# A linear-attention and feed-forward kernel on one Trainium2 core: its static order, early transfers, early engines and feed-forward leads planned anew

## The chip, the cores and the metric

The kernel runs on one core of a Trainium2 chip. Its time is the device time of one execution in microseconds (us); the time before is the median of three runs. The engines are named as in the profile: PE (TensorE matmul), PEld (its weight loads), DVE (VectorE), ACT (ScalarE), POOL (GpSimd) and SP, whose queue starts the loads.

## What is computed

```python
def _attn_ref(q, k, v, alpha):              # each (4, 8, 768, 48)
    for t in range(S):
        state = alpha[:, :, t, :, None] * state + np.einsum('bhd,bhe->bhde', k[:, :, t], v[:, :, t])
        y[:, :, t] = np.einsum('bhd,bhde->bhe', q[:, :, t], state)
def _moe_ref(x, w1, w2, w3, w_out):         # x: (3072, 384) from y; w: (384, 768), w_out: (768, 384)
    h = np.maximum(np.maximum(x @ w1, x @ w2), x @ w3)
    return h @ w_out
```

All inputs and the output are float32.

## The kernel before

**Units.** The 768 positions are cut into 6 blocks of 128, and with 4 batches that makes 24 units (u); a unit has 8 heads of 48. Two units form a group n (12 groups), which shares its loads: four inputs a, q, k, v of 384 KB each (alpha, q, k, v), in five rotating buffers (`load`, L383).

**Attention of a unit** (`prep` L519, `output` L607, `state` L665). ACT takes the logarithm of alpha (L489); PE sums it over the block with a triangular matrix (L530); ACT takes two exponentials, ep and en (L533, L535). q times ep and k times en go to a 16-bit tile qk (L542, on POOL or DVE), v is scaled to 16 bits (L548 on ACT or L553 on POOL). PE turns q and k with eight transposes (L563), DVE copies them out of PSUM (L567), PE forms the scores (L575), DVE masks them (LA, L580), PE adds up the output (L618, L621), ACT scales it to xb (L638), PE turns xb (L645) and DVE copies it to xT (L649). The state is carried by L676 (PE), L682 (DVE) and L689 (DVE in the first block, POOL later).

**Feed-forward of a group** (`ffn`, L698). Since max(x w1, x w2, x w3) = x w1 + max(max(x (w2 - w1), x (w3 - w1)), 0) up to the order of terms, the kernel keeps wd = w2 - w1 and w3 - w1 (`subs`, L437) and the folded product w1 w_out (w1o; PE turns w1 in L454, multiplies in L471, ACT copies). PE multiplies wd with xT (L714; 36 matmuls of 128x256 a group), ACT applies relu (L724), DVE takes the maximum (L729), PE multiplies with w1o and w_out (L745; 9 matmuls of 128x384 a unit), ACT copies the result (L755) and starts its store (L756).

**The order.** No engine's order is written out by hand. Every operation is a `plan.step` with an engine, a cost, a rank, what it reads and writes, and for loads a transfer time (`load=`). `Plan.order` (L173) runs these steps once in a model of the engines, the transfers (`Transfers`, L52), the PSUM banks and PE's clock (`Clock`, L93): at each moment the step that can start first is taken, among equals that of the lowest rank. The result is the static order of each engine's queue; on the chip, an engine runs its queue strictly in that order and waits where an input is late. Units have rank u; group n's feed-forward has rank 2n + LEAD (L31, L702), so a larger lead lets attention go first. The constants at the head steer it: EARLY (L32) names the engines for q, k and v of the first units (POOL where nothing is said), SUBS (L37) those of the subtractions, WCUTS (L36) the pieces in which each weight matrix is loaded, FIRST (L39) the order of the first transfers on SP's queue, WARM (L46, `warm` L652) a number of matmuls on zeros that keep PE busy, PAIRS (L47) the unit from which the scores of two units are run as one step.

Of the kernel before, what the change touches and what calls it, by code (L numbers as in the profile page):

```python
# [10 lines left out]
FP32 = mybir.dt.float32  # L11
# [19 lines left out]
LEAD = 5.0  # L31
EARLY = {0: ("POOL", "POOL", "POOL"), 1: ("DVE", "POOL", "ACT"), 2: ("DVE", "DVE", "POOL"),  # L32
         3: ("DVE", "POOL", "POOL"), 4: ("POOL", "DVE", "POOL"), 5: ("DVE", "DVE", "ACT"),
         6: ("POOL", "POOL", "POOL"), 7: ("DVE", "POOL", "ACT"), 8: ("POOL", "DVE", "POOL")}
WEIGHTS = ()
WCUTS = (0, 256, 512, 768)  # L36
SUBS = {(1, 0): "POOL", (1, 1): "DVE", (1, 2): "DVE", (2, 0): "POOL", (2, 1): "POOL",  # L37
        (2, 2): "POOL"}
FIRST = (("a", 0, 0, 1), ("w", 1, 0), ("q", 0, 0, 1), ("a", 0, 1, 2), ("w", 0, 0),  # L39
         ("k", 0, 0, 1), ("q", 0, 1, 2), ("w", 1, 1), ("k", 0, 1, 2), ("w", 2, 0), ("w", 0, 1),  # L40
         ("v", 0, 0, 1), ("v", 0, 1, 2), ("w", 2, 1), ("w", 1, 2), ("a", 1, 0, 1),
         ("q", 1, 0, 1), ("w", 2, 2), ("w", 0, 2), ("k", 1, 0, 1), ("akq", 1, 1, 2),
         ("w", 3, 1), ("w", 3, 0), ("v", 1, 0, 1), ("w", 3, 2), ("v", 1, 1, 2),
         ("aqkv", 2, 0, 2), ("aq", 3, 0, 1), ("q", 3, 1, 2), ("k", 3, 0, 1), ("a", 3, 1, 2),
         ("v", 3, 0, 1), ("v", 3, 1, 2), ("k", 3, 1, 2))
WARM = (2, 1, 9)  # L46
PAIRS, CROSS = 8, 99  # L47
TURNED, PAUSE = 3.5, 0.3
# [3 lines left out]
class Transfers:  # L52
# [6 lines left out]
    def add(self, e, arrival, work, i, late):  # L59
        self.jobs[e].append([arrival, work, i, late])  # L60

# [55 lines left out]
class Plan:  # L117
# [12 lines left out]
    def step(self, eng, cost, rank, run, reads=(), writes=(), banks=(), load=0.0, line=None,  # L130
             mode=0, late=0.0, after=0.0):
        i = len(self.steps)
        deps = set()
        if line is not None:
            if line in self.tail:
                self.behind[i] = self.tail[line]
            self.tail[line] = i
        for k in reads:
            if k in self.writer:
                deps.add(self.writer[k])  # L140
        for k in writes:
            if k in self.writer:
                deps.add(self.writer[k])
            deps.update(self.readers.get(k, ()))
        for k in reads:
            self.readers.setdefault(k, []).append(i)
        for k in writes:
            self.writer[k] = i
            self.readers[k] = []
        deps.discard(i)  # L150
        for k in set(reads) | set(writes):
            if k in self.users:
                self.users[k].append(i)
        for k in banks:
            self.users[k] = [i]
        self.steps.append((eng, cost, rank, run, deps, tuple(banks), load, mode, late, after))
# [16 lines left out]
    def order(self):  # L173
# [23 lines left out]
        dma, mode = Transfers(), 0  # L197
# [17 lines left out]
        while len(seq) < n:  # L215
            best = None
            for e, cand in pending.items():
                pick = None
                for i in cand:
                    at = self.homes(bank_free, self.steps[i][5])  # L220
                    if at is None:
                        continue
                    t = max(ready[i], free[e], at[0])
                    turn = TURN_RANK if e == "PE" and self.steps[i][7] != mode else 0.0
                    key = (t, self.steps[i][2] + turn, i)
                    if pick is None or key < pick:
                        pick = key
                if pick is not None and (best is None or pick < best[0]):
                    best = (pick, e)
            landing = dma.next()  # L230
# [6 lines left out]
            _, cost, _, _, _, banks, load, m, late, after_ = self.steps[i]  # L237
# [12 lines left out]
            if load:  # L250
                dma.add(e, t + cost + DMA_IN[e], load, i, late)
            else:
                finish(i, t + cost + HOP[e] + after_)
# [7 lines left out]
def kernel(  # L261
# [30 lines left out]
    NX = 6  # L292
# [42 lines left out]
    xTs = homes(NX, [P, NFT, TG], FP16, "xT")  # L335
    hTs = homes(3, [P, NJ, TG], FP16, "hT")
# [46 lines left out]
    def load(n, lo, hi, names="aqkv"):  # L383
        cb, g = divmod(n, B // UB)
        for x in names:
            t = ld[x][n % 5]

            def run(x=x, t=t):
# [6 lines left out]
                      load=(1.84 if n < 3 else 2.02 if n < CROSS // 2 else 2.02 + PAUSE) * (hi - lo) / HG,  # L395
# [21 lines left out]
    def wload(g, part):  # L417
# [6 lines left out]
                  load=3.2 * (WCUTS[part + 1] - WCUTS[part]) / DF)  # L424
# [93 lines left out]

    def prep(u):  # L519
# [39 lines left out]
        def trans():  # L559
            live[tk] = bank(tk, [P, 2, NP, P], FP16)  # L560
            for w in range(2):
                for j in range(NP):
                    nc.tensor.transpose(live[tk][:, w, j, :], qk[:, w, 2 * j:2 * j + 2, :], ident)  # L563

        plan.step("PE", 0.45, u, trans, banks=[tk],
                  reads=[("qk", u % 7, 0), ("qk", u % 7, 1)], writes=[tk, ("qkT room", u % 3)])
        plan.step("DVE", 0.69, u, lambda: nc.vector.tensor_copy(out=qkT, in_=live[tk]),  # L567
                  reads=[tk], writes=[("qkT", u % 3)])
# [38 lines left out]
    def output(u):  # L607
# [20 lines left out]
        if u >= CROSS:  # L628
            def across():
                nc.scalar.activation(out=xb, in_=live[yk].rearrange("p a b -> p (a b)"),  # L630
                                     func=AFT.Copy, scale=ysc)
                nc.scalar.dma_start_transpose(out=xTs[n % NX][:, :, i * P:(i + 1) * P], in_=xb)

            plan.step("ACT", 0.93, u, across, reads=[yk], after=TURNED,
                      writes=[("xb", u % 5), ("xT", n % NX, i)])
            return
# [3 lines left out]
                  reads=[yk], writes=[("xb", u % 5)])  # L640

        def turn():
            live[xk] = bank(xk, [P, NFT, P], FP16)
            for ft in range(NFT):
# [4 lines left out]
                  lambda: nc.vector.tensor_copy(out=xTs[n % NX][:, :, i * P:(i + 1) * P], in_=live[xk]),  # L649
                  reads=[xk], writes=[("xT", n % NX, i)])  # L650

    def warm(u, w, count):  # L652
        live["wm"] = None

        def zeros():
            live["wm"] = bank(("wm", 0), [P, TG], FP32)
            nc.tensor.matmul(live["wm"], Zs[1][0].rearrange("p a b -> p (a b)")[:, :P],
                             Zs[1][0].rearrange("p a b -> p (a b)")[:, :TG], start=True, stop=True)

        for i in range(count):  # L660
            plan.step("PE", 0.11, 90.0, zeros, banks=[("wm", 0)] if i == 0 else [], line="warm",
                      reads=[("qk", u % 7, w)] if i == 0 else [],
# [35 lines left out]
    def ffn(n):  # L698
        cb, g0 = divmod(n, B // UB)
        xT, hT = xTs[n % NX], hTs[n % 3]  # L700
        npieces = 2 * (NJ // 2) + UB
        rank = [2 * n + LEAD + 2.0 * i / npieces for i in range(npieces)]  # L702
        for j in range(NJ // 2):
            parts = parts_of(j)
            for g in range(2):
                r = rank[2 * j + g]
                gk = ("gp", n, j, g)

                def grow(j=j, g=g, gk=gk):
                    live[gk] = bank(gk, [P, 2, TG], FP32)  # L710
                    for jj in range(2):
                        c0 = (2 * j + jj) * P
                        for kt in range(NFT):
                            nc.tensor.matmul(live[gk][:, jj, :], wd[:, kt, g, c0:c0 + P],  # L714
                                             xT[:, kt, :], start=(kt == 0), stop=(kt == NFT - 1))

                plan.step("PE", 0.656, r, grow, banks=[gk],
                          writes=[gk] + ([("room", n % 3, j)] if g == 0 else []),
                          reads=[("room", n % 3, j)] * (g > 0)
                          + [("wd", g + 1, p) for p in parts] + [("xT", n % NX, 0), ("xT", n % NX, 1)])  # L720
                h = hT[:, 2 * j:2 * j + 2, :]
                if g == 0:
# [3 lines left out]
                              reads=[gk], writes=[("hT", n % 3, j)])  # L726
                else:
                    plan.step("DVE", 0.69, r,
                              lambda h=h, gk=gk: nc.vector.tensor_max(h, live[gk], h),  # L729
                              reads=[gk, ("hT", n % 3, j)], writes=[("hT", n % 3, j)])  # L730
        for i in range(UB):
            b = g0 * UB + i
            m = n * UB + i
            r = rank[2 * (NJ // 2) + i]
            ok = ("op", m)
            nk = NFT + NJ
            parts = [(0, nk)] if n < NG - 1 else [(0, nk - 2), (nk - 2, nk)]
            for lo, hi in parts:
                def shrink(i=i, ok=ok, lo=lo, hi=hi):
                    if lo == 0:  # L740
                        live[ok] = bank(ok, [P, DM], FP32)
                    for kt in range(lo, hi):
                        a, w = ((xT[:, kt], w1o[:, kt]) if kt < NFT
                                else (hT[:, kt - NFT], wo16[:, kt - NFT]))
# [5 lines left out]
                          reads=[(x, n % 3, j) for x in ("hT", "room")  # L750
                                 for j in range(max(0, lo - NFT) // 2, (hi - NFT) // 2)]
                          + [("xT", n % NX, i)] + [("w", 3, p) for p in range(nparts)] + [("w1o", kt) for kt in range(NFT)])
# [5 lines left out]
            plan.step("ACT", 0.9, r, leave, reads=[ok], writes=[("ob room", m % 4)])  # L758


    for what, n, lo, *hi in FIRST:
# [4 lines left out]
        else:  # L766
            load(n, lo * H, hi[0] * H, what)
    made = dict.fromkeys(SUBS, False)
    for n in range(NG):
# [21 lines left out]
        if n >= 4:  # L791
            ffn(n - 4)
    for n in range(NG - 4, NG):
        ffn(n)
# [35 lines left out]
```

## Time and profile before

| what | us |
|---|---|
| median of 3 runs (156.71 to 157.77) | 157.55 |
| the profiled execution | 157.7 |
| its span, first to last instruction | 155.9 |
| PE busy | 137.4 |
| DVE busy | 100.6 |
| ACT busy | 86.7 |
| POOL busy | 73.6 |
| last load landed (v of the last group) | 115.95 |
| last matmul ended | 151.6 |
| mean granted TensorE clock | 0.989 |

Times in the trace count from the start of the span; 1.8 us of the execution lie outside it. 23.69 MB are read and 4.72 MB written. A row of the timeline or of the groups names the line, the engine, the operation, the tiles it writes and reads, and in brackets the idle time of the engine ahead of it with what ended it.

### The profile page before, as it was taken

The page shows a single profiled execution, that of the slowest core. Times are in us where ns is not written, and L with a number is a line of the kernel's source. Part 1 is how long each engine was busy: PE and PEld are TensorE (multiplying, and loading weights), DVE is VectorE, ACT ScalarE, POOL GpSimd, SP SyncE. Part 2 cuts the span into 40 slices and gives each one's busy share as a digit, 9 for nine tenths or more (in the row PEclk, how much of TensorE's full clock was granted, in tenths as well). Part 3 has the DMA queues.
Part 4 walks back from the last instruction along what each step waited for, and adds up shares of the span by engine and source line. Part 5 has one row for each costly group of instructions (what it writes and reads, how often), then busy time and mean ns, then how long its engine had stood idle before and what let it go on. Part 6 is the DMA issues. An engine that isn't in the chain of part 4 may idle for free.

```text
span 155.9 us, 4070 instructions
## 1 busy us (share of the span) xinstructions
PE 137.4 (88%) x1621; PEld 106.8 (69%) x1621; DVE 100.6 (65%) x171; ACT 86.7 (56%) x175; POOL 73.6 (47%) x100
## 2 busy tenths in 40 slices
PE   0255695999999999999999999999999999999990
PEld 0133464676787797697787887787887877968750
DVE  7035529862998799873969685695884975833220
ACT  3462664679578583487366477284682653525221
POOL 0268704322144077597979548668469483000000
PEclk9999999599999999999999999999999999999999
DMA  5999998999998999998999989999961102011202
GB/s 139 247 277 290 290 294 176 320 204 229 191 236 172 220 254 178 231 276 167 249 254 201 269 184 240 231 217 197 269 136 53 48 4 101 4 50 50 87 13 101
DMA packets 107442, 28.66 MB, mean 184 GB/s; under 512 B 100000, under 2 KB 107424, under 8 KB 107424
## 3 DMA queue, kind: packets, MB, share of 16 engines
q1 hardware_dynamic: 103680, 23.60, 72.9%
q10 hardware_dynamic: 3744, 4.82, 8.9%
q8 instruction: 12, 0.20, 0.5%
q14 instruction: 6, 0.05, 0.1%
HBM read 23.69 MB, written 4.72 MB: 182 GB/s over the span
## 4 chain that ended last, share of the span: by engine, by line
PE 68%; DMA 12%; SPq 11%; ACT 2%; issue 2%; POOL 1%; DVE 1%; ACTq 0%; POOLq 0%
PE psum L714 26%; PE psum L745 19%; DMA an<-in_alpha_dram 7%; SPq L419 7%; PE psum L563 5%; DMA vn<-in_v_dram 4%; SPq L389 4%; PE psum L575 4%; PE psum L621 2%; PE psum L645 2%; PE psum L530 2%; PE psum L676 2%; PE psum L618 2%; POOL qk L542 1%; PE psum L502 1%
## 5 line engine op out<-in xcount | busy, mean ns | idle before, releaser
L714 PE MATMUL psum<-xT,wd 128*128 128x256 f16 x432 | 57.8, 283 | 0.0
L714 PEld LDWEIGHTS <-wd 128*128 128x128 f16 x432 | 42.0, 101 | 8.0 <-issue 1.0
L542 POOL TENSOR_TENSOR qk<-qn,ep 128x384 f16<-128x384 f32 x19 | 19.0, 1000 | 27.4 <-ACT ep L533 21.3
L580 DVE TENSOR_TENSOR LA<-psum,c 128x1024 f16<-128x1024 f32 x24 | 28.6, 1219 | 4.6 <-PE psum L575 4.6
L729 DVE TENSOR_TENSOR hT<-psum,hT 128x512 f16<-128x512 f32 x36 | 24.4, 687 | 10.9 <-PE psum L714 6.3
L724 ACT ACTIVATE hT<-psum 128x512 f16<-128x512 f32 x36 | 21.2, 603 | 13.1 <-PE psum L714 12.5
L745 PE MATMUL psum<-wo,hT 128*128 128x384 f16 x144 | 27.3, 326 | 0.0
L542 POOL TENSOR_TENSOR qk<-kn,en 128x384 f16<-128x384 f32 x20 | 20.0, 1000 | 7.6 <-ACT en L535 4.2
L755 ACT COPY ob<-psum 128x384 f32<-128x384 f32 x24 | 11.5, 478 | 20.9 <-PE psum L745 20.4
L567 DVE COPY qkT<-psum 128x1024 f16<-128x1024 f16 x24 | 16.4, 688 | 9.6 <-ACT ob L755 7.1
L745 PEld LDWEIGHTS <-hT 128*128 128x128 f16 x144 | 14.1, 98 | 9.3
L553 POOL TENSOR_SCALAR v<-vn,c 128x384 f16<-128x384 f32 x21 | 13.0, 622 | 13.6 <-DMA vn<-in_v_dram 12.2
L489 ACT ACTIVATE la<-an 128x768 f16<-128x768 f32 (+1 forms) x15 | 10.7, 715 | 14.0 <-DMA an<-in_alpha_dram 13.6
L563 PE MATMUL psum<-c,qk 128*128 128x128 f16 x192 | 16.2, 227 | 1.9 <-DVE qk L542 1.4
L689 POOL TENSOR_TENSOR Z<-U,G 48x192 f16<-48x192 f32 x32 | 15.7, 505 | 2.1 <-DVE U L682 1.2
L638 ACT ACTIVATE xb<-psum,c 128x384 f16<-128x384 f32 x24 | 13.8, 584 | 3.9 <-PE psum L621 2.2
L745 PE MATMUL psum<-w1o,xT 128*128 128x384 f16 x72 | 15.6, 326 | 0.0
L563 PEld LDWEIGHTS <-qk 128*128 128x128 f16 x192 | 12.6, 101 | 4.2 <-DVE qk L542 1.6
L533 ACT ACTIVATE ep<-psum 128x384 f32<-128x384 f32 x24 | 11.8, 494 | 4.4 <-PE psum L530 4.4
L649 DVE COPY xT<-psum 128x384 f16<-128x384 f16 x24 | 8.4, 353 | 7.5 <-PE psum L645 7.4
L530 PE MATMUL psum<-la,c 128*128 128x384 f16 x24 | 8.3, 345 | 4.6 <-ACT la L489 4.6
L621 PE MATMUL psum<-v,LA 128*128 128x48 f16 x192 | 11.5, 186 | 0.9 <-DVE LA L580 0.8
(41 smaller groups left out, 155.4 us busy)
## 6 DMA issues: line engine op xcount, KB each, us to landing
out_dram<-ob ACTq DMA_DIRECT2D x24, 192.0 KB, 3.1
ws<-in_moe_w_dram SPq DMA_DIRECT2D x9, 384.0 KB, 4.7
an<-in_alpha_dram SPq DMA_DIRECT2D x9, 384.0 KB, 6.1
qn<-in_q_dram SPq DMA_DIRECT2D x9, 384.0 KB, 6.3
kn<-in_k_dram SPq DMA_DIRECT2D x9, 384.0 KB, 5.6
vn<-in_v_dram SPq DMA_DIRECT2D x9, 384.0 KB, 6.4
an<-in_alpha_dram SPq DMA_DIRECT2D x6, 192.0 KB, 4.7
qn<-in_q_dram SPq DMA_DIRECT2D x6, 192.0 KB, 4.5
```

Of the source, the lines that this page charges most:

```text
L542: nc.gpsimd if eng == "POOL" else nc.vector).tensor_mul(
L553: lambda: nc.gpsimd.tensor_scalar(out=v16, in0=ld["v"][n % 5][:, hs], scalar1=vsc, scalar2=1.0, op0=AOP.mult, op1=AOP.mult),
L563: nc.tensor.transpose(live[tk][:, w, j, :], qk[:, w, 2 * j:2 * j + 2, :], ident)
L567: plan.step("DVE", 0.69, u, lambda: nc.vector.tensor_copy(out=qkT, in_=live[tk]), reads=[tk], writes=[("qkT", u % 3)])
L580: lambda: nc.vector.tensor_mul(LA.rearrange("p a b t -> p (a b) t"), live[Ak].rearrange("p a (b t) -> p (a b) t", t=P), maskA.unsqueeze(1) ...
L621: nc.tensor.matmul(yp[:, 2 * j + p, :], LA[:, p, j, :], v16[:, 2 * j + p, :], start=(cb == 0), stop=True, skip_group_check=True)
L638: lambda: nc.scalar.activation(out=xb, in_=live[yk].rearrange("p a b -> p (a b)"), func=AFT.Copy, scale=ysc),
L689: eng.tensor_mul(Zn[rows, :, cols], U[rows, :, cols], G[rows, i * NP:(i + 1) * NP].unsqueeze(2).broadcast_to([D, NP, D]))
L714: nc.tensor.matmul(live[gk][:, jj, :], wd[:, kt, g, c0:c0 + P], xT[:, kt, :], start=(kt == 0), stop=(kt == NFT - 1))
L724: lambda h=h, gk=gk: nc.scalar.activation(out=h, in_=live[gk], func=AFT.Relu),
L729: lambda h=h, gk=gk: nc.vector.tensor_max(h, live[gk], h),
L745: nc.tensor.matmul(live[ok], a[:, i * P:(i + 1) * P], w, start=(kt == 0), stop=(kt == nk - 1))
```

## The change

It alters the constants that steer the order, some costs in the planner's model, and how feed-forward work is cut into calls. The operations, their shapes and their number stay, but for the weights' pieces (three a matrix become two, so twelve transfers, six casts and six subtractions become eight, four and four) and the matmuls on zeros (9 of 256 columns become 12 of 384, put early and no longer after unit 2's k). The weight pieces in `FIRST` are reordered among those of a, q, k and v: both halves of q and a of group 0 come first, and w3 comes last. All subtractions run on DVE. The q and k products of units 1, 3 and 5 to 10 that go to DVE, and the v of units 8 to 10 that go to ACT, are chosen anew. Scores run in pairs from unit 12, not 8. The feed-forward lead 5.0 becomes 6.0 for the first call, 9.0 for the second and 7.0 for all others. The planner charges a store to the transfers (`store`), adds 1.0 us of other traffic at 24.5 us and every 11 us after, and costs a load of a group at 1.82 us each.

`turn_in` is the old code for turning q and k, moved into a function of its own. The new branches for turning by a transfer (`cross`, and the one in `output`) apply to units from 24 on, of which there are none; `WIDE` is 99, so feed-forward calls stay at two units. xT is held in 3 tiles of four units, not in 6 of two.

```diff
-LEAD = 5.0
-EARLY = {0: ("POOL", "POOL", "POOL"), 1: ("DVE", "POOL", "ACT"), 2: ("DVE", "DVE", "POOL"),
-         3: ("DVE", "POOL", "POOL"), 4: ("POOL", "DVE", "POOL"), 5: ("DVE", "DVE", "ACT"),
-         6: ("POOL", "POOL", "POOL"), 7: ("DVE", "POOL", "ACT"), 8: ("POOL", "DVE", "POOL")}
+LEAD = (6.0, 9.0, 7.0)
+EARLY = {1: ("POOL", "DVE", "POOL"), 3: ("DVE", "DVE", "POOL"), 4: ("POOL", "POOL", "POOL"),
+         5: ("DVE", "POOL", "POOL"), 6: ("DVE", "DVE", "POOL"), 7: ("POOL", "DVE", "POOL"),
+         8: ("POOL", "DVE", "ACT"), 9: ("POOL", "DVE", "ACT"), 10: ("POOL", "DVE", "ACT"),
+         11: ("POOL", "POOL", "POOL")}
-WCUTS = (0, 256, 512, 768)
-SUBS = {(1, 0): "POOL", (1, 1): "DVE", (1, 2): "DVE", (2, 0): "POOL", (2, 1): "POOL",
-        (2, 2): "POOL"}
-FIRST = (("a", 0, 0, 1), ("w", 1, 0), ("q", 0, 0, 1), ("a", 0, 1, 2), ("w", 0, 0),
-         ("k", 0, 0, 1), ("q", 0, 1, 2), ("w", 1, 1), ("k", 0, 1, 2), ("w", 2, 0), ("w", 0, 1),
-         ("v", 0, 0, 1), ("v", 0, 1, 2), ("w", 2, 1), ("w", 1, 2), ("a", 1, 0, 1),
-         ("q", 1, 0, 1), ("w", 2, 2), ("w", 0, 2), ("k", 1, 0, 1), ("akq", 1, 1, 2),
-         ("w", 3, 1), ("w", 3, 0), ("v", 1, 0, 1), ("w", 3, 2), ("v", 1, 1, 2),
+WCUTS = (0, 384, 768)
+SUBS = {(1, 0): "DVE", (1, 1): "DVE", (2, 0): "DVE", (2, 1): "DVE"}
+FIRST = (("aq", 0, 0, 1), ("aq", 0, 1, 2), ("k", 0, 1, 2), ("w", 0, 0), ("v", 1, 0, 1),
+         ("k", 0, 0, 1), ("k", 1, 0, 1), ("w", 0, 1), ("qa", 1, 0, 1), ("w", 1, 1),
+         ("w", 1, 0), ("v", 0, 0, 1), ("v", 0, 1, 2), ("k", 1, 1, 2), ("a", 1, 1, 2),
+         ("w", 3, 1), ("q", 1, 1, 2), ("w", 3, 0), ("w", 2, 0), ("v", 1, 1, 2), ("w", 2, 1),
...
-WARM = (2, 1, 9)
-PAIRS, CROSS = 8, 99
+WARM = (0, 0, 12)
+PAIRS, WIDE = 12, 99
+CROSS_IN, CROSS_OUT = 24, 24
+FETCH, FETCHES, STORE = 1.0, (24.5, 11.0), 0.3
...
+    def store(self, work):
+        if self.jobs["SP"]:
+            self.jobs["SP"][0][1] += work
...
-                      load=(1.84 if n < 3 else 2.02 if n < CROSS // 2 else 2.02 + PAUSE) * (hi - lo) / HG,
+                      load=1.82 * (hi - lo) / HG,
...
-                  load=3.2 * (WCUTS[part + 1] - WCUTS[part]) / DF)
+                  load=3.25 * (WCUTS[part + 1] - WCUTS[part]) / DF)
...
-    xTs = homes(NX, [P, NFT, TG], FP16, "xT")
+    xTs = homes(NX, [P, NFT, B * P], FP16, "xT")
...
-        rank = [2 * n + LEAD + 2.0 * i / npieces for i in range(npieces)]
+        rank = [u0 + LEAD[min(f, 2)] + k * i / npieces for i in range(npieces)]
```

In `FIRST`, an entry such as ("aq", 0, 0, 1) loads a and q of group 0, first unit of the two; ("w", 2, 1) loads the second piece of w3 (w1, w2, w3 and w_out count as 0 to 3).

## The prediction

> **What bounds the kernel now.** I read the page first: busy times, then the 40 slices.
>
> ```profile
> PE 137.4 (88%) x1621; PEld 106.8 (69%) x1621; DVE 100.6 (65%) x171; ACT 86.7 (56%) x175; POOL 73.6 (47%) x100
> ...
> PE   0255695999999999999999999999999999999990
> ...
> PEclk9999999599999999999999999999999999999999
> DMA  5999998999998999998999989999961102011202
> ```
>
> TensorE (PE) is full from slice 8 to the end; before that it waits, while the DMA engines are full from slice 2 until slice 29. So the kernel has two parts: a start of about 31 us whose pace is that of the transfers, and 120 us in which PE never rests. The stretches say how complete that is (columns: length, then busy time and instructions of PE, weight loads, DVE, ACT, POOL, then granted clock, DMA share, GB/s).
>
> ```profile
> 20.00:25.00 5.00, 4.32 (x23) 2.95 (x22) 1.94 (x3) 2.80 (x5) 1.34 (x1) 1.00 1.19 282
> 25.00:27.00 2.00, 1.07 (x16) 0.90 (x17) 2.00 (x3) 0.82 (x3) 0.29 (x1) 1.00 0.52 118
> 27.00:30.00 3.00, 3.00 (x22) 1.89 (x21) 2.74 (x5) 1.81 (x4) 0.99 (x1) 0.53 1.08 336
> 40.00:50.00 10.00, 10.00 (x139) 8.07 (x136) 8.66 (x17) 7.19 (x16) 3.81 (x5) 1.00 1.00 212
> 60.00:70.00 10.00, 9.68 (x124) 7.60 (x122) 8.40 (x14) 6.58 (x14) 7.25 (x13) 1.00 1.24 247
> ```
>
> After 40 us PE is idle for 0.7 us in all, up to the last matmul at 151.6. What the end is made of, then, is the column of PE's work plus what PE has lost by the time it is full. Third, the timeline, for how the start loses time:
>
> ```profile
> 20.23 3.87 PE L714 MATMUL psum<-xT,wd 128*128 128x256 f16 x18
> ...
> 23.71 2.00 DVE L542 TENSOR_TENSOR qk<-kn,en 128x384 f16<-128x384 f32 x1 [2.16 <-DMA kn<-in_k_dram]
> ...
> 25.76 0.40 PE L563 MATMUL psum<-c,qk 128*128 128x128 f16 x4 [1.45 <-DVE qk L542]
> ...
> 26.68 2.27 PE L714 MATMUL psum<-xT,wd 128*128 128x256 f16 x12
> ...
> 31.43 1.15 PE L657 MATMUL psum<-Z 128*128 128x256 f16 x9
> ```
>
> The 18 matmuls at 20.2 stand 0.213 us apart; later ones 0.109. PE ran at half rate until 23.8, fast to 27.2, at half rate to 30.6, then fast for good. The nine matmuls on zeros cost 0.98 us at 31.4, when PE already has work. Last, the groups of DVE (count | busy, mean ns of one | idle before), because the change gives it more to do:
>
> ```profile
> L580 DVE TENSOR_TENSOR LA<-psum,c 128x1024 f16<-128x1024 f32 x24 | 28.6, 1219 | 4.6 <-PE psum L575 4.6
> L567 DVE COPY qkT<-psum 128x1024 f16<-128x1024 f16 x24 | 16.4, 688 | 9.6 <-ACT ob L755 7.1
> ```
>
> **The change, part by part.** The sum is made against the profiled execution: 157.7 us, span 155.9, so 1.8 outside the span; it stands 0.15 above the median.
>
> PE's useful column is the same in both orders: adding up steps (6 feed-forward matmuls 0.656, 9 output ones 1.46, a unit's transposes 0.45, scores 0.28, and so on, all from the chain of waits) gives 124.9 us without the zeros. Regrouping the x-transposed buffers (6 of 256 columns into 3 of 512) keeps every matmul's shape: 0. "All q and k turned on TensorE" changes nothing either: 192 transposes stand in the profile now, 24 units by 8. PAIRS 8 to 12 splits two pairs of score groups: a pair takes 0.55, two singles 0.33 each, so +0.11 each, +0.2 in all. I therefore follow both orders to one common point, then to a second, then to the end.
>
> *First point.* When unit 4's first cumulative sum starts, both orders have done the same PE steps (36 feed-forward matmuls, all 18 of the folded product, units 0 to 3). Before: 36.8 us. For the new order I list landings. In the trace, pieces of 192 KB land 0.84 us apart, weights of 384 KB 1.22 (rows of 1 KB) or 1.13 to 1.18 (w_out, rows of 1.5 KB), so a 576 KB piece takes about 1.73 (1.70 to 1.83). Two bumps of 0.9 and 1.0 us between 24 and 33 are kept. From the first landing at 3.6: alpha 0 and 1 at 3.6 and 5.8, q 4.9 and 6.6, k of unit 1 at 7.5, w1 9.2 and 13.4, k of unit 0 at 10.9, w2 16.8 and 18.6, v 19.4 and 20.2, alpha of unit 3 at 21.9, w_out 23.7 and 27.1, w3 28.9 and 32.4. The same bytes are in at 33.2 now; twelve weight pieces at 1.2 against eight at 1.73 is 0.6 less, the rest the order of the bumps.
>
> Along these landings: the twelve zero matmuls run from 7.1 to 11.4, where PE waits for transfers; cost 0. The feed-forward work of the first two units begins at 24.6, at half rate (PE too idle between 17 and 23 to keep its clock), its first 12 matmuls end at 27.2. w_out's second half (27.1) waits on ACT behind two relus (to 27.8), its cast of 1.2 us ends at 29.0, so the folded product starts at 29.1. Then DVE is last: copy of unit 3's q and k 29.2 to 29.9, first w3 subtraction to 31.3, mask of unit 3 to 32.5, second w3 subtraction (landed 32.4) to 33.9. These subtractions are the part that moves: six (four on POOL at 1.64, two on DVE at 0.95) become four on DVE, at 0.95 x 1.5 = 1.4 each, so DVE has +3.7 us, POOL -6.9. Twelve feed-forward matmuls follow, 34.0 to 35.3. The common point comes at 35.3: 1.5 us earlier.
>
> *Second point.* Between 36 and 51 us nothing is left to fill PE. Unit 4 and 5's outputs are needed before a third feed-forward group can start, and the two before it are used up. DVE then has, for units 4 to 6, three masks (1.2), three copies (0.69), maxima (0.69), four q/k products, eight state products and two small ones: some 16 us, and it must wait about 2.2 us in between for PE (the output matmuls ahead of the first state sums at 38.0, the second group's matmuls at 40.5). Unit 6's mask ends at 51.2 if each duration counts whole, 50.8 if neighbours overlap as two masks in 2.36 us do now; PE's column alone would be there at 49.2. Now, at the same place in the column, PE stands at 51.0. So 1.5 us is given back almost whole: -1.3 (bounds: -1.7 with no overlap, 0 if PE has other work). I take -1.3, the overlapping value, as the row has it. What waits behind is PE's unit 7 transposes.
>
> *From 51 to the end.* Now PE loses 2.7 us there beyond its column: 0.7 idle, the rest little by little at changes of step. In the new order the output of unit 8 comes at about 63.0 (with the same small losses) against 63.7. Later units are turned 4 to 8 us earlier in the column (the three leads are longer, so 21.9 us of feed-forward stands behind the last attention output, 16.2 now). That must meet the loads: tightest is unit 20, wanted at 102.5, its alpha in use at 102.0 if the stream is 0.8 earlier than now; for the last k there are 6 us of margin, and ACT, POOL and SP queues have theirs with it. I take 0.4 for stalls (0 to 1.5), a gain of 1.0 over this part with the 0.2 for PAIRS inside.
>
> Sum: 1.5 - 1.3 + 1.0 = 1.2, rounded down to 1.1 for what single waits I did not see. Span 154.8, execution 156.6, median 156.5 us.
>
> [...] The trace: between 23.8 and 27.2 PE was busy for 1.6 of 3.4 us, and the next 3.4 us were at half rate (granted 0.53). [...]
>
> **The rivals.** (A) *DVE is not late.* If the second w3 half lands by 31.4 and DVE's neighbours overlap more, the -1.3 falls away: 1.5 + 1.0 = 2.5, so 155.0 us. For it: DVE has 35% spare over the span. Against: 8.66 busy of 10 between 40 and 50 already.
>
> (B) *The last weight is late; slower.* The w3 half is the last of 24 transfers, and its subtraction, the maxima, the output and state steps and unit 4 to 6's masks follow in one line with no filler. Now w3 is complete at 18.5 and w_out at 32.3, which has ACT behind it, not DVE. Each us past 32.4 is a us on the end. Single transfers did come 1.4 us late (alpha at 25.8, again at 52.0). With three such bumps (4.2) in place of the two kept (1.9), and weights at 1.83 (+0.8), it lands at 35.5: 3.1 more than the forecast, so 159.6 us. It decides against "before" from a landing of 33.5.
>
> (C) *The clock comes late.* The half-rate windows end at 23.8, 27.2, 30.6 in this execution. Were the last switch to fast at 30.6, not 27.2, some 2 us of PE's work there would take twice as long, 0.9 of it in waits: +1.1, 157.6 us. [...]
>
> (D) *Nothing changes.* The planner's costs move, but the DMA-bound start and the PE column stay: 157.5. Against: 1.2 us of PE zeros and half-rate stretches are demonstrably gone or moved.
>
> **How the numbers follow.** Forecast (gain 0.5 to 1.8, 155.7 to 157.0) 0.36; A 0.25; B 0.25 (158.5 to 160.5); C 0.10; D 0.04. The likeliest is 156.5. The range to hold 8 in 10 reaches into A and B: 154.8 to 159.6. A measurement of this kernel tells about 1% from no change: below 156.0 is faster, above 159.1 slower. Faster: A and a tenth of the forecast's case, 0.29; slower: three quarters of B, 0.19; same 0.52.
>
> **What would show it.** Zero matmuls between 7 and 11.5 and PE at full rate by about 10, half rate again near 17 to 27; unit 4's cumulative sum at 35.3 (36.8 now); the second w3 half landing at 32.4 with its subtraction right behind on DVE; PE idle 1 to 2 us between 43 and 52, released by DVE (masks, q/k products); afterwards under 1 us idle to the end. Wrong if the w3 half lands past 33.5, if PE is idle over 2 us after 52, or if no DVE wait stands in 43 to 52.

## The result and the profile after

The changed kernel takes 158.33 us (median of 11 runs, 157.20 to 158.96); the kernel before took 157.07 in 11 runs beside it (156.71 to 158.08). The ratio is 1.006, interval 1.004 to 1.009: slower by 0.6%, inside the 1% that the prediction calls no change, but on the other side of it from the forecast of 156.5. The profiled execution took 158.57 us, its span 156.8 (155.9 before).

From the page after:

```profile
PE 139.5 (89%) x1624; PEld 107.2 (68%) x1624; DVE 103.9 (66%) x174; ACT 86.4 (55%) x173; POOL 68.3 (44%) x95
...
PE   0577538999998999999999999999999999999990
...
PEclk9999999999999999999999999999999999999998
```

DVE has 3.3 us more and POOL 5.3 less (forecast +3.7 and -6.9). The agreement is not as good as it looks: the four subtractions brought DVE 5.0 us more, not 3.7, and part of that is offset by cheaper q and k products (6.7 us on DVE, 8.0 before). PE now starts work early (the zeros, slices 2 to 4) and then waits. PEclk must be read with care: this trace has no clock record before 29.3 us, and the row fills the gap with nines; the spacing of the matmuls below (0.21 us, where it is 0.109 later) says half rate.

Three of the same stretches (length, then busy time and instructions of PE, weight loads, DVE, ACT, POOL, then clock, DMA share, GB/s):

```profile
20.00:25.00 5.00, 2.35 (x28) 1.60 (x26) 4.04 (x4) 0.99 (x2) 4.00 (x3) 1.00 1.06 233
...
40.00:50.00 10.00, 9.62 (x132) 7.29 (x129) 8.45 (x16) 5.62 (x13) 3.79 (x6) 1.00 1.03 222
60.00:70.00 10.00, 10.00 (x143) 8.21 (x140) 7.33 (x13) 7.39 (x17) 5.05 (x8) 1.00 1.08 241
```

From 20 to 25 us PE is busy for 2.35 us (4.32 before), DVE for 4.04 and POOL for 4.00 of five. At 40 to 50 PE has begun to wait, at 60 to 70 it no longer does. DVE's masks (L601) and copies have kept their mean durations (1216 and 685 ns; 1219 and 688 before); the subtractions (L446) take 1747 ns in the mean, where 1.4 us was forecast:

```profile
L601 DVE TENSOR_TENSOR LA<-psum,c 128x1024 f16<-128x1024 f32 x24 | 28.6, 1216 | 7.4 <-PE psum L596 7.4
...
L446 DVE TENSOR_TENSOR wd<-ws,w1h 128x1152 f16<-128x1152 f32 x4 | 6.9, 1747 | 1.1 <-DMA ws<-in_moe_w_dram 1.1
```

To compare the orders I use PE's loss: the time of a point less the useful matmul work that PE has begun before it (the step durations of the prediction's column, zeros not counted). From the two traces:

| point | before | after | gain | forecast |
|---|---|---|---|---|
| unit 4's first cumulative sum: time | 36.76 | 37.06 | -0.3 | +1.5 |
| loss there | 23.56 | 23.86 | -0.3 | +1.5 |
| loss from there to 56 us | 0.68 | 1.88 | -1.2 | -1.3 |
| loss from 56 us to the end | 2.53 | 1.91 | +0.6 | +1.0 |

The three gains sum to -0.9, the difference of the spans. The second step came out nearly as forecast, the third at half its size or better; the first did not. This is where it went, on the timeline of after (start, duration, engine, line; the idle time in brackets):

```profile
18.71 1.00 POOL L563 TENSOR_TENSOR qk<-qn,ep 128x384 f16<-128x384 f32 x1 [6.26 <-ACT ep L554]
18.77 4.22 DVE L446 TENSOR_TENSOR wd<-ws,w1h 128x1152 f16<-128x1152 f32 x2 [1.11 <-DMA ws<-in_moe_w_dram]
19.66 2.11 POOL L563 TENSOR_TENSOR qk<-kn,en 128x384 f16<-128x384 f32 x1
21.76 2.25 POOL L574 TENSOR_SCALAR v<-vn,c 128x384 f16<-128x384 f32 x2
23.50 0.48 PE L642 MATMUL psum<-v,LA 128*128 128x48 f16 x8 [1.06 <-POOL v L574]
27.11 2.53 PE L735 MATMUL psum<-xT,wd 128*128 128x256 f16 x12
30.17 1.14 ACT L437 CAST wo<-ws 128x1152 f16<-128x1152 f32 x1
34.17 1.34 DVE L446 TENSOR_TENSOR wd<-ws,w1h 128x1152 f16<-128x1152 f32 x1
```

Two subtractions take 4.22 us where the single one at 34.17 takes 1.34, and POOL's k product 2.11 where the q product took 1.00: the two engines stand in each other's way, and unit 0's output waits for POOL's v behind them. The first feed-forward matmuls start at 27.11 (forecast 24.6), twelve in 2.53 us, 0.21 apart: half rate. The landings are late as well (from the trace's transfers): w_out at 26.1 and 29.8 (forecast 23.7 and 27.1), w3 at 31.4 and 33.8 (28.9 and 32.4), alpha of unit 3 at 24.4 (21.9). The eight 576 KB pieces landed 2.42, 2.70, 2.35, 1.66, 1.66, 2.92, 1.68 and 1.58 us after the transfer ahead of them; I had 1.73 for each.

### The profile page after: what moved, and what is told of

Same layout as the page of the kernel before. It is cut to its first block, busy times and chain, and to the rows that moved or that the text cites. A ratio compares the mean times of both kernels' runs of the same rounds, so it can differ in the third digit from the quotient of the medians.

```text
span 156.8 us, 4054 instructions
## 1 busy us (share of the span) xinstructions
PE 139.5 (89%) x1624; PEld 107.2 (68%) x1624; DVE 103.9 (66%) x174; ACT 86.4 (55%) x173; POOL 68.3 (44%) x95
## 4 chain that ended last, share of the span: by engine, by line
PE 73%; SPq 6%; DVE 6%; issue 4%; DMA 3%; POOL 3%; ACT 2%; ACTq 0%; POOLq 0%
PE psum L735 28%; PE psum L768 22%; PE psum L533 5%; SPq L398 5%; PE psum L596 3%; DMA qn<-in_q_dram 3%; PE psum L642 3%; DVE LA L601 2%; PE psum L639 2%; PE psum L480 2%; PE psum L664 2%; POOL qk L563 2%; PE psum L551 2%; PE psum L694 2%; POOL v L574 1%
## 5 line engine op out<-in xcount | busy, mean ns | idle before, releaser
L735 PE MATMUL psum<-xT,wd 128*128 128x256 f16 x432 | 55.4, 276 | 0.2
L735 PEld LDWEIGHTS <-wd 128*128 128x128 f16 x432 | 41.1, 99 | 7.1 <-issue 0.5
L563 POOL TENSOR_TENSOR qk<-qn,ep 128x384 f16<-128x384 f32 x21 | 20.9, 999 | 34.5 <-ACT ep L554 31.6
L601 DVE TENSOR_TENSOR LA<-psum,c 128x1024 f16<-128x1024 f32 x24 | 28.6, 1216 | 7.4 <-PE psum L596 7.4
L574 POOL TENSOR_SCALAR v<-vn,c 128x384 f16<-128x384 f32 x21 | 14.3, 685 | 15.7 <-DMA vn<-in_v_dram 15.5
L563 POOL TENSOR_TENSOR qk<-kn,en 128x384 f16<-128x384 f32 x17 | 18.4, 1088 | 0.2
(40 smaller groups left out, 156.4 us busy)
```

The costliest lines, as they stand in the source:

```text
L563: nc.gpsimd if eng == "POOL" else nc.vector).tensor_mul(
L574: lambda: nc.gpsimd.tensor_scalar(out=v16, in0=ld["v"][n % 5][:, hs], scalar1=vsc, scalar2=1.0, op0=AOP.mult, op1=AOP.mult),
L601: lambda: nc.vector.tensor_mul(LA.rearrange("p a b t -> p (a b) t"), live[Ak].rearrange("p a (b t) -> p (a b) t", t=P), maskA.unsqueeze(1) ...
L735: nc.tensor.matmul(live[gk][:, jj, :], wd[:, kt, g, j * P:(j + 1) * P], xT[:, kt, :], start=(kt == 0), stop=(kt == NFT - 1))
```

## Experiments

Theory L: the late landings alone set the first point. Theory C: the contention of DVE and POOL, with PE at half rate, does. Theory D: from 47 to 51 us PE waits for DVE. "Contention" here means that an instruction on DVE and one on POOL hold each other up. After the first four runs theory J took the place of L and C: both chains end at nearly the same time. Ratios below are to the kernel before on the same chip, with 95% intervals; times inside a trace are of one execution, and landings of the same order differed between executions: the second piece of w1 was in at 14.84 in after, at 15.5 in the run with the light load below. "The sum" is the start of unit 4's first cumulative sum.

### Landings, zeros and maxima, one at a time

The zeros left out:

```diff
-            nc.tensor.matmul(live["wm"], zero[:, :P], zero, start=True, stop=True)
```

> The changed kernel in its own order, with the twelve matmuls on zeros left out (they feed nothing). Theory L (the start is set by when the weight pieces land: w_out's second half at 29.8, w3's at 33.8 in the changed kernel's trace): the zeros ran where PE waits and never won the clock, so unit 4's cumulative sum stays at 37.1 within 0.4 and the time at 158.3 within 0.4. Theory C (the start is set by PE at half rate until 29.3 and by DVE and POOL slowing each other): the zeros are part of what could win the clock in other executions, so without them the time rises by 0.5 to 1.5, or falls by as much if they delay unit 1's transposes.

Measured 1.004 (1.000 to 1.007), unit 4's sum at 37.35: the early zeros bring nothing that the time shows. What they do to the clock differs between executions of the same kernel. In 8 of the 11 of the changed kernel the mean granted clock is 0.956 to 0.965 (median 157.95 us), in 3, the profiled one among them, about 0.996 (158.57); the times of the two groups overlap. What the means stand for is read from the matmuls of the traces. In the light load below, with a mean of 0.965, twelve transposes of w1 take 0.84 us from 16.85 on, and four of q and k at 19.73 take 0.61, where four at full rate take 0.40 (at 29.69 in the run with 19 zeros below): full rate early, then half; by the mean, the half rate comes to about 11 us in all (an estimate: 2 x 0.035 x 156.4). In after, with 0.996, the twelve transposes of w1 take 1.46 from 16.33 on. Without the zeros the mean was 0.996 to 1.000 in all 12 executions.

Each weight piece as three transfers:

```diff
+                  lambda: [nc.sync.dma_start(
+                      piece(wst[g], g, part)[:, t], ...[:, t]) for t in range(3)],
```

> The changed kernel in its own order, each weight piece of 576 KB moved by three transfers of 192 KB (same bytes, same rows of 1.5 KB). Theory L, in the form that SP's queue stands behind one large piece (issues of 2.7, 2.8 and 3.5 us at 7.0, 11.8 and 16.5): the stalls shorten, unit 3's alpha lands before 23.5 (24.4 now), w3 before 33.0 (33.8), unit 4's sum starts 0.7 to 1.5 earlier than 37.1 and the time falls to 157.0 to 157.6. Theory L in the form that the engines are simply full, and theory C: landings within 0.4, time 158.3 within 0.4.

Measured 1.004 (1.001 to 1.007). Only the two pieces of w1 came 0.3 to 0.4 us sooner; w_out landed later still (27.9 and 30.1, against 26.1 and 29.8 in after), its second cast stood behind two relus until 31.27, and the sum came at 38.20. Neither form of theory L foresaw that. That large pieces hold up the queue is refuted; why some land 1 us late stays open.

A third of w_out loaded:

```diff
+                      piece(wst[g], g, part)[:, :1 if g == 3 else 3],
```

> The changed kernel in its own order, but each of the two w_out pieces loads only one third of its rows (768 KB less in all; the rest keeps w1's values, so the output is not the reference's). Theory L: w_out's second piece lands by 28 (29.8), w3's by 32 (33.8), and unit 4's sum starts about 1.8 earlier, at 35.3; if DVE then holds PE in 43 to 52 as before, part of it (0.5 to 1) is given back, time 157.0 to 157.6; if not, 156.5. Theory C: unit 4's sum at 36.7 or later, time 158.0 or more.

Measured 1.001 (0.997 to 1.005). w_out was in at 28.4 and w3 at 32.5, both 1.3 earlier, and the sum stood at 37.02 as in after. On its timeline:

```profile
19.28 3.68 DVE L446 TENSOR_TENSOR wd<-ws,w1h 128x1152 f16<-128x1152 f32 x2 [1.10 <-DMA ws<-in_moe_w_dram]
...
27.07 2.53 PE L735 MATMUL psum<-xT,wd 128*128 128x256 f16 x12
...
30.14 1.14 ACT L437 CAST wo<-ws 128x1152 f16<-128x1152 f32 x1
```

The cast of w_out begins where it did in after, 1.7 us past its landing, since it stands on ACT behind relus of the late matmuls. Theory L falls.

The maxima of the first two feed-forward groups left out:

```diff
+                              lambda h=h, gk=gk: None if f < 2 else nc.vector.tensor_max(h, live[gk], h),
```

> The changed kernel in its own order, with DVE's maxima of the first two feed-forward groups left out (six of 0.69; those groups' hidden values are then those of w2 alone, so the output is not the reference's). Theory D (between 47 and 51 PE waits for DVE, which has no slack because nothing fills PE): PE's loss between useful columns 20 and 27, 1.7 now, falls to 0.6 or less, and the time by 1.0 to 1.5, to about 157.0. Rival (it waits there for loads or POOL, DVE is only named last): loss and time stay within 0.4.

Measured 1.002 (0.999 to 1.005). Between the sums of units 6 and 8 PE loses 0.85 us, against 1.44 in after, 1.15 to 1.20 in the three runs above and 0.2 in the kernel before. Theory D asked for more: a loss of 0.6 or less and a time near 157.0; the time shows no gain that can be told. The maxima are thus worth 0.3 to 0.6 of the loss. Without them DVE waits for PE's scores ahead of its masks, and is busy almost without a break from there to PE's wait:

```profile
44.79 2.39 DVE L601 TENSOR_TENSOR LA<-psum,c 128x1024 f16<-128x1024 f32 x2 [0.23 <-PE psum L596]
```

So DVE is late, as theory D has it, but by its masks, products and copies more than by its maxima. The section on the second point shows where the spread from 1.15 to 1.44 comes from.

### Contention taken away, and both taken away

Unit 2's k product goes to DVE, the second w2 subtraction behind the copy of unit 2's turned q and k, the v of units 0 and 1 to ACT:

```diff
-                          nc.gpsimd if eng == "POOL" else nc.vector).tensor_mul(
+                          nc.gpsimd if eng == "POOL" and (u, x) != (2, "k") else nc.vector).tensor_mul(
+                      lambda: nc.scalar.activation(out=v16, in_=ld["v"][n % 5][:, hs], func=AFT.Copy, scale=vsc)
+                      if u < 2 else nc.gpsimd.tensor_scalar(...),
+        seq.remove(x); seq.insert(seq.index(y) + 1, x)
```

> The kernel after the change, with its order kept but for this: unit 2's k product moves from POOL to DVE, ahead of the two subtractions for w2; the second subtraction moves behind the copy of unit 2's turned q and k; the v of units 0 and 1 is scaled on ACT. So no POOL product runs beside a w2 subtraction except unit 2's q. Theory J (two chains end at nearly the same time at the first point: one through the slowed subtractions and products to the first feed-forward group, one through the landings of w_out at 29.8 and w3 at 33.8): each subtraction takes 1.35 to 1.6, the first feed-forward matmuls (L735) start at 25.6 (27.11 after), but the cast of w_out can move only 0.4 and the last w3 subtraction 0.3, so unit 4's first cumulative sum starts at 36.7 (37.06): gain 0.4 at most, time ratio to before 1.002 to 1.006. Theory C (the contention alone sets the first point): sum at 35.6 to 36.0, ratio 0.995 to 1.0. Theory N (neither; half-rate PE): sum unchanged within 0.2.

```profile
18.63 0.99 POOL L563 TENSOR_TENSOR qk<-qn,ep 128x384 f16<-128x384 f32 x1 [5.68 <-ACT ep L554]
18.97 1.07 DVE L563 TENSOR_TENSOR qk<-kn,en 128x384 f16<-128x384 f32 x1 [1.07 <-ACT en L556]
19.96 1.35 DVE L446 TENSOR_TENSOR wd<-ws,w1h 128x1152 f16<-128x1152 f32 x1
...
21.84 1.34 DVE L446 TENSOR_TENSOR wd<-ws,w1h 128x1152 f16<-128x1152 f32 x1
...
26.75 2.61 PE L735 MATMUL psum<-xT,wd 128*128 128x256 f16 x12
```

The subtractions now take 1.35 each, and the k product, put beside POOL's q product, 1.07 instead of 0.55: still one after the other. Measured 1.002 (0.998 to 1.005), sum at 36.85, 0.2 earlier: theory C alone falls too. PE waits 0.86 us for alpha of unit 3 (landed 24.7), and the first feed-forward matmuls still start at 26.75, at half rate.

The same with the light w_out:

> As the run with the contention taken away, and w_out loaded to a third only (two thirds of w_out's rows are left out of the load, so the output is another), by which w_out and w3 land 1.3 earlier (w_out's second piece at 28.4, w3's at 32.5). Theory J: the w_out cast starts at 28.5 (30.17), the folded product at 29.8 (31.4), the last w3 subtraction at 32.6 to 33.0 (34.17), unit 4's sum at 35.4 to 35.7: a gain of 1.4 to 1.6, although the light load alone gained nothing and the calm order alone at most 0.4; ratio 0.994 to 1.0. Theory C: as the calm order alone, within 0.3. Theory N: within 0.3 of 37.06.

Measured 0.997 (0.993 to 1.001), sum at 36.04: 1.0 earlier, where the two edits alone gave 0.04 and 0.2. That is theory J, short of its 1.4. What is left is PE at half rate (its first 12 matmuls take 2.37 us). So two runs have in addition alpha of unit 3 ahead of k of unit 3, and 19 matmuls on zeros in PE's gaps:

```diff
+    fill = lambda key, n: [nc.tensor.matmul(bank(key, [P, DM], FP32), zero[:, :P], zero, ...) for _ in range(n)]
+    seq.remove(marks["a", 1, H]); seq.insert(seq.index(marks["k", 1, H]), marks["a", 1, H])
```

> As the run with alpha moved ahead and two products on POOL, and 19 matmuls on zeros put where PE waits between 17.8 and 26 us (6 ahead of unit 2's transposes, 5 and 3 ahead of units 0's and 1's outputs, 3 ahead of unit 0's transposed output, 2 ahead of unit 3's totals). If PE stays fast through them, the first 12 feed-forward matmuls take 1.3 (2.6 in the calm run). Theory J: w_out at 29.9 and w3 at 34.0 set the first point all the same, sum at 36.6 to 36.8. Theory H (half-rate PE sets it): sum at 35.4 to 35.9. Cost if the zeros win no clock and stand in the way: up to 0.8 at the first point. Ratio to before by J: 0.995 to 1.0; by H 0.988 to 0.993.

```profile
25.88 1.47 PE L735 MATMUL psum<-xT,wd 128*128 128x256 f16 x12 [0.29 <-DVE xT L668]
...
27.03 1.15 ACT L437 CAST wo<-ws 128x1152 f16<-128x1152 f32 x1 [1.80 <-DMA ws<-in_moe_w_out_dram]
...
28.72 0.34 PE L664 MATMUL psum<-c,xb 128*128 128x128 f16 x3 [1.37 <-ACT xb L650]
...
30.26 1.18 ACT L437 CAST wo<-ws 128x1152 f16<-128x1152 f32 x1
```

PE is at full rate (1.47 for the twelve), and the sum comes at 37.18, no earlier: 1.002 (0.997 to 1.007). w_out's first half landed at 27.0; ACT waits for it with unit 2's output behind, and PE waits 1.37 us for that output. With the light w_out, without that wait:

> The calm order with alpha of unit 3 ahead, the 19 zero matmuls, and w_out loaded to a third only (two thirds of its rows left out, so the output is another). Theory J with the half rate as its third part: now w_out's cast starts at 27.6 (29.15 in the calm run with the light load, where half-rate matmuls and two relus stood before it), the folded product at 28.8 (30.35), the last w3 subtraction at its landing, 31.8 (33.15), unit 4's sum at 34.5 to 34.9 (36.04). If the half rate has no part: 35.7 to 36.1. If even this stays at 36.0 although PE is fast, another link is open.

```profile
25.42 1.47 PE L735 MATMUL psum<-xT,wd 128*128 128x256 f16 x12 [0.29 <-DVE xT L668]
...
28.12 1.18 ACT L437 CAST wo<-ws 128x1152 f16<-128x1152 f32 x1
```

Measured 0.986 (0.981 to 0.991), sum at 35.05. The four corners, time of unit 4's sum:

| | w_out whole | w_out a third |
|---|---|---|
| order of after | 37.06 | 37.02 |
| no contention, alpha earlier, PE kept fast | 37.18 | 35.05 |

Either obstacle by itself holds the first point; only both taken away together give 2.0 us. The lower row takes away three things at once. With the light w_out, the contention is 1.0 of the 2.0 (37.02 to 36.04); alpha and the rate of PE are the other 1.0 (to 35.05), and no run tells these two apart.

### The second point

Two products go from DVE to POOL:

```diff
+                          ... or (u, x) in ((6, "q"), (7, "k"))
```

> The calm order (unit 2's k product on DVE, second w2 subtraction later, v of units 0 and 1 on ACT) with two more edits: alpha of unit 3 is loaded ahead of k of unit 3, and the q product of unit 6 and the k product of unit 7 go from DVE to POOL. First point, theory J: alpha of unit 3 lands at 23.2 (24.7 in the calm run), L735 starts at 25.6 (26.75), but w_out (29.9) and w3 (34.0) land as before, so unit 4's sum stays at 36.7 to 36.9; if alpha alone set it, the sum is at 35.7. Second point, theory D (PE waits for DVE with nothing to fill): PE's loss between unit 4's sum and 52 us falls from 1.75 to 0.9 to 1.3; if DVE is not what is late, or POOL's slower products (1.0 to 2.1) are late instead, it stays at 1.6 or more. Time ratio to before by J and D: 0.996 to 1.0.

Alpha of unit 3 was moved here as well, and it came to 23.4; the sum was at 37.12, as J has it. Measured 0.997 (0.993 to 1.001); PE lost 1.17 us between the sums of units 6 and 8, no less than the 1.15 of the light load. Up to 52 us, the measure of the expectation, the loss fell from 1.75 to about 1.5: not the 0.9 to 1.3 of theory D. The move gave back on DVE what it took off:

```profile
47.19 1.00 POOL L563 TENSOR_TENSOR qk<-qn,ep 128x384 f16<-128x384 f32 x1 [4.33 <-ACT ep L554]
47.56 1.04 DVE L563 TENSOR_TENSOR qk<-kn,en 128x384 f16<-128x384 f32 x1
```

The k product on DVE, now beside POOL's q product, takes 1.04. In after it was a v on POOL that stood in DVE's way:

```profile
45.24 2.34 DVE L601 TENSOR_TENSOR LA<-psum,c 128x1024 f16<-128x1024 f32 x2
47.36 0.59 POOL L574 TENSOR_SCALAR v<-vn,c 128x384 f16<-128x384 f32 x1 [4.94 <-DMA vn<-in_v_dram]
47.51 0.85 DVE L563 TENSOR_TENSOR qk<-qn,ep 128x384 f16<-128x384 f32 x1
48.28 0.55 DVE L563 TENSOR_TENSOR qk<-kn,en 128x384 f16<-128x384 f32 x1
...
49.31 0.69 DVE L537 COPY qkT<-psum 128x1024 f16<-128x1024 f16 x1
...
50.06 0.40 PE L596 MATMUL psum<-qkT 48*128 48x128 f16 x8 [0.28 <-DVE qkT L537]
```

DVE has no gap over 0.15 us from 45.2 to PE's wait at 50.06; the q product took 0.85 beside the v. In the run with the light load no v stood there, the same product took 0.55, and PE lost 0.29 less: that is the whole spread from 1.44 to 1.15.

### Parts of the change, planned anew

The changed kernel with the start's constants of before (`EARLY`, `FIRST`, `WCUTS`, `SUBS`, `WARM`), then the kernel before with those of after:

```diff
-WCUTS = (0, 384, 768)
+WCUTS = (0, 256, 512, 768)
...
-WARM = (0, 0, 12)
+WARM = (2, 1, 9)
```

> The kernel after the change with the start's constants of before (EARLY, FIRST, WCUTS, SUBS, WARM), planned anew: the leads, PAIRS and the planner's costs are the new part. If the new start is what made the change slower and the longer leads are worth about 0.7 to 1.0 after 51 us: unit 4's first sum near 36.8, and time 0.5 to 1.0 below before (ratio 0.993 to 0.998). If the leads give back what they gain (no filler between 36 and 51 us): ratio 0.999 to 1.004.

> The kernel before with the start's constants of after (EARLY, FIRST, WCUTS, SUBS, WARM), planned anew: lead 5.0 and PAIRS 8 as before. If the new start costs 0.3 at unit 4's sum, and the loss between 36 and 51 us comes from the longer leads: sum at 37.0, little lost to 51, end as before: ratio 1.0 to 1.003. If the loss between 36 and 51 us comes from the new engines for q, k and v (EARLY) or from w3 being late: it shows here too, and without the gain of the leads the ratio is 1.007 to 1.013.

The new leads with the old start: 1.000 (0.996 to 1.004); loss from the sum to 56 us 1.08, after it 2.42. The new start with the old lead: 1.017 (1.012 to 1.022); 1.11 and 4.56. Both had their sum at 38.2 to 38.4, so they say nothing on the first point. But the new start with short leads loses 4.56 at the end, and with long leads 1.91: with this start the longer leads are worth it, with the old start next to nothing (2.42 against 2.53 in the kernel before). Each plan is another order throughout, so this compares four orders, not two parts by themselves.

Before without its nine zeros at 31.4:

```diff
-            nc.tensor.matmul(live["wm"], Zs[1][0]...[:, :P], Zs[1][0]...[:, :TG], start=True, stop=True)
```

> The kernel before with its nine zero matmuls at 31.4 left out, order kept otherwise. The prediction counted their 0.98 us as time that the new order saves. If that is so: unit 4's sum at 35.8 (36.76), ratio 0.992 to 0.996. If they stand where PE waits for the cast of w_out (landed 32.3) and for the subtractions: sum within 0.2 of 36.76, ratio 0.998 to 1.002. If they keep the clock: ratio above 1.002.

Measured 0.998 (0.994 to 1.003), sum at 37.26, no earlier than 36.76: the 0.98 us were no cost that can be told. In both traces the folded product starts 0.6 to 0.7 us after the last cast of w_out has begun (at 32.34 in before, at 32.98 here), zeros or not.

### Another order of the landings

w_out, then k and q of unit 3, then w3, then v of unit 3, with all bytes:

```diff
+    late = [marks[x] for x in (("w", 3, 1), ("w", 3, 0), ("k", 1, H), ("q", 1, H), ("w", 2, 0), ("w", 2, 1), ("v", 1, H))]
```

In a first form of these three kernels w_out's load stood ahead of the casts of w1 that read the same buffer, so that w1 was cast from w_out's rows; they took 173 to 175 us and answer nothing. In the second form it stays behind them.

> The calm order, alpha of unit 3 ahead, two products on POOL, the 19 zeros, and the last seven transfers of the start in the order w_out (both), k and q of unit 3, w3 (both), v of unit 3; w_out's load stays behind both casts of w1. All work and all bytes are there. If the order of the landings is the other part (with contention and the half rate): w_out lands at 25.5 and 27.2 (27.0 and 29.5 in the run with zeros and the old order), its second cast ends at 29.5 to 30.0 (31.4), the folded product starts at 29.7 to 30.1 (31.5), w3's second piece lands at 32.5 (33.7), unit 4's sum at 35.3 to 36.0 (37.18): ratio to before 0.988 to 0.995. If the bytes themselves bound the start, w3 still lands at 33.5 and the sum stays at 36.5 or later.

> As the run with the order of landings, calm order and zeros, but without the 19 zeros. If the half rate has a part of its own: the first 12 feed-forward matmuls take 2.6 (1.5 with the zeros), unit 4's sum 0.6 to 1.2 later than with them, near 36.5. If not: within 0.3 of it.

> The kernel after with only the transfers reordered (alpha of unit 3 ahead of the rest, then w_out, k and q of unit 3, w3, v of unit 3); engines and the order of the other work as after. If contention holds the start too (theory J): w_out is in at 27 but the first feed-forward matmuls still start at 26.5 or later at half rate and the relus stand on ACT ahead of the second cast, unit 4's sum at 36.3 to 36.9, ratio 0.999 to 1.004. If the landing order alone set it: 35.3 to 36.0.

Measured 1.006 (1.002 to 1.010), 1.003 (0.999 to 1.007) and 1.011 (1.005 to 1.017): no gain. In the first, w_out (25.5, 27.1), its second cast (28.71) and the second w3 subtraction (33.30) all came as hoped, but a new wait took the gain:

```profile
33.30 1.35 DVE L446 TENSOR_TENSOR wd<-ws,w1h 128x1152 f16<-128x1152 f32 x1
...
33.52 1.58 POOL L575 TENSOR_SCALAR v<-vn,c 128x384 f16<-128x384 f32 x1 [14.62 <-DMA vn<-in_v_dram]
...
35.15 0.36 PE L642 MATMUL psum<-v,LA 128*128 128x48 f16 x8 [1.87 <-POOL v L575]
```

The v of unit 3, put last, landed at 33.4; POOL scaled it beside the subtraction, in 1.58 instead of 0.59, and PE waited 1.87 for it. The sum came at 37.80; less that wait it would be 35.9, by this estimate. With v ahead of w3's last piece it might be had; that was not tried. The third run met the same wait (1.86 us, v landed at 34.9) and had its sum at 39.48, where 36.3 to 36.9 was expected. The second run, without the 19 zeros, is not slower than the first. No version with all the work beats the kernel before by more than its interval; the nearest is the calm order with alpha earlier and two products on POOL (0.997).

## Why the prediction was wrong

*First point: the step that failed.* "The common point comes at 35.3: 1.5 us earlier" came out at 37.06. The chain was the right one: with contention, half rate and late landings all taken away it gave 35.05 (with only a third of w_out loaded). Two terms in it were mis-sized, each enough by itself to hold the first point.

- The landings: 1.73 us for a 576 KB piece, with two bumps. The eight took 16.97 us in all, 2.12 on average: four came in 1.58 to 1.68 us, the other four in 2.35 to 2.92, three of these before 19 us, where no bump was allowed for. w_out was 2.7 late and w3 1.4. Why they came late is open.
- The cost of moving the subtractions. I took 1.4 each, which a single one does take, and nothing for what POOL does at that moment: beside POOL's products the two take 4.22, POOL's k product 2.11 and its two v 2.25 (0.59 each alone). The first feed-forward matmuls came 2.5 late; part of that is alpha of unit 3, which landed 2.5 late itself (without the contention they still start at 26.75). In the prediction POOL's 6.9 us less work stood only as relief.

The price could be read before the change. The k product at 23.71, which the prediction shows, took 2.00 us on DVE where it takes 0.55 alone; on POOL a subtraction had begun 0.05 us ahead of it. The mean of its group was 1193 ns:

```profile
23.66 1.64 POOL L437 TENSOR_TENSOR wd<-ws,w1h 128x768 f16<-128x768 f32 x1 [4.61 <-ACT w1h L428]
```

```profile
L542 DVE TENSOR_TENSOR qk<-kn,en 128x384 f16<-128x384 f32 x4 | 4.8, 1193 | 3.0 <-DMA kn<-in_k_dram 2.2 <-ACT e L508 0.8
```

The runs of the changed orders agree: on DVE a product of 0.55 becomes 1.04 to 1.07 beside a POOL product of 1.00, and 0.85 beside a v of 0.59. The two rows of before above spoke against the change, and I did not weigh them.

The zeros: "PE at full rate by about 10" was my estimate, and was not so in the profiled execution, where seven of the twelve zeros took 2.45 us from 6.72 on, 0.32 apart; in 8 of 11 the mean clock points to an early stretch of full rate. What sets the one or the other was not shown. It mattered little: kept at full rate by the 19 zeros (five of them in 0.98 us at 20.65, 0.16 apart; then the first 12 feed-forward matmuls in 1.47, against 2.72 in the same order without them), PE was no earlier at the first point (37.18). So rival C (the clock comes late) happened as well, full rate from 29.3 by the trace's first clock record, and by itself cost nothing that the first point shows. Between 23.8 and 27.2 in the kernel before, PE was busy for 1.8 us, not 1.6; the half rate of the next 3.4 us (granted 0.50) stays as told.

*Second point: right.* Forecast -1.3, measured -1.2. Unit 6's mask ends 15.4 us after the first point (37.06 to 52.43), where 15.5 was forecast, and PE waits for DVE at 50.06, DVE being full, as said. What was not foreseen is that 0.3 of it is a collision with POOL. One sign was off: by its busy time PE is idle for 0.56 us between 43 and 52, not 1 to 2; the rest of the loss is matmuls that start a little late one by one.

*To the end: right in sign.* Forecast +1.0, measured +0.6; of the four orders planned, only the one with both the new start and the longer leads gains clearly there.

*Rivals.* B (last weight late, slower) described the direction, but not the mechanism: w3's second piece landed at 33.8, a little past the 33.5 at which B decides, yet earlier landings alone changed nothing. (B's 18.5 for w3 in the kernel before is the landing of w2; w3 was complete at 21.5.) Against D I held that 1.2 us of zeros and half rate were "demonstrably gone or moved"; leaving the zeros out of the kernel before gained nothing that can be told.

## What to carry to other kernels

Before moving work to an engine with spare time, look at what its neighbour does in the same microseconds: here a DVE subtraction and a POOL product side by side took 2.15 and 2.11 us, where alone they take 1.35 and 1.00, so each about the sum of both. A group whose mean is far above what one instruction takes alone (1193 ns against 547) is the sign to look for. When several chains of a stage end at nearly the same time, taking one away gains next to nothing; forecast it by the second-latest chain, and test causes in pairs. A transfer's time scaled up from smaller pieces was near the best case here: half of the eight pieces took 0.6 to 1.2 us longer, so allow for bumps piece by piece.

## What the runs showed of the hardware

DVE's products and subtractions and POOL's products and scalings ran for the most part one after the other. On DVE a subtraction of 128x1152 took 1.35 us alone and up to 2.15 beside POOL, a product 0.55 to 2.00; on POOL a product took 1.00 to 2.21, a v 0.58 to 1.80. The masks on DVE (LA<-psum,c) took 1.21 to 1.23 in either kernel. Equal 576 KB pieces landed 1.58 to 2.92 us behind the transfer ahead of them, and three transfers of 192 KB in place of each were not sooner in, but for the first two pieces (by 0.3 to 0.4). With matmuls on zeros at 6.7 to 13.3 us the mean granted clock was 0.956 to 0.965 in 8 of 11 executions of one kernel and 0.996 in the other 3; without them it was 0.996 to 1.000 in 12 of 12. In the traces of the light load, of the calm order and of the two together (means 0.964 and 0.965) a cumulative sum at 17.27 to 17.58 took 0.32 us, and the transposes of q and k that began at 19.43 to 19.73 took 1.03 for eight or 0.61 for four (0.82 and 0.40 at full rate); in that of the changed kernel, with 0.996, the same sum took 0.53.
